# Three moves in one kernel: late sums of squares, expert weights in freed blocks, a gather ahead of scatters

## The chip, the cores and the metric

The kernel runs on one core of a Trainium2 chip. The metric is the device time of one execution in microseconds: the median over runs, here 1042.28 us before the change (three runs, 1041.61 to 1044.61).

## The reference

Three stages follow each other; the output of one is the input of the next.

```python
# 1 attention with decay: 4 batches, 8 heads, 576 positions, 64 wide
scores = q @ k.T / 8 + cum[:, None] - cum[None, :]   # cum = cumsum(log f), causal
x = softmax(scores) @ v                              # 2304 tokens of 512
# 2 SwiGLU, 1536 wide
x = (silu(x @ w_gate) * (x @ w_val)) @ w_out
# 3 one of 8 experts for each token, 1024 wide
e = argmax(x @ r_gate);  out = prob[e] * (relu(x @ w1[e]) @ w2[e])
```

All of it is float32, and the kernel splits operands into a high and a low part so that three cheaper products stand for one.

## The kernel before, in words

**Attention and SwiGLU run interleaved.** Attention is cut into 64 slots (4 batches, 4 pairs of heads, 4 slots to a pair). A slot computes scores for one item (`part1`), narrows the probabilities of the item before and sends them through a DMA transpose (`part2`, tile `pt`), and multiplies the item before that with v (`pv`, tile `px`). SwiGLU is cut into 54 units: 9 groups of 256 tokens, 6 column blocks of 256 to a group. A unit makes the gate product (`g`, 24 matmuls), the value product (`v`, 24 matmuls) and, for the unit before, the output product (`yp`, 12 matmuls). `pace` says how many slots are laid out by each unit.

**The scale of v.** Before v is narrowed to two float16 parts it is scaled by a power of two, found for a whole batch from the sum of its squares. `v_scale(b)` (line 795) loads the batch in four pieces (`vr`), squares them on ACT with a running sum (`sq`), and then calls `pow2_scale` (line 772): four matmuls `tot<-sq` on PE that add the sums over all partitions, and four small operations on DVE, through one of the three score buffers in PSUM. It is called in the 11th slot of the batch before (line 449), and `prep_v` uses the scale in the 14th.

**The gate and value weights** are kept as float16 pairs in two tiles, `wg16` and `wv16`, six blocks each. Blocks 4 and 5 also serve as landing room for raw weights while they are not yet filled.

**Routing.** After each group `fin0` copies the result `yp` to `ys` and writes it to `y_d` in DRAM. `fin1` transposes it. `fin2` finds each token's expert, its rank there, and the tables `ixf` and `ix` of token numbers by expert slot. `put_ids` scatters the numbers of tokens beyond an expert's 320 places to `id_d`, by two indirect DMAs issued from POOL; the second waits until the first has landed, since both write `id_d`. The small tiles `pos` and `tid`, which hold the scatter's addresses and values, have one buffer each that all groups share. For the last group they are copied to tiles of their own and scattered later.

**The early part of expert 0.** When group 7 of the nine (0 to 8) is routed, expert 0 surely has 128 tokens. `early_tile` (line 966) gathers them from `y_d` (tile `xg`, indirect DMA from POOL), PE transposes them into `px`, and `filler` (line 990) runs this tile through expert 0 in pieces while the last group is routed.

**Expert weights** come in eight chunks of 512 KB per expert, four for each matrix, into four landing buffers `wr`. A chunk's buffer is free again when ACT has written its high part and DVE its low part (`load_w`, lines 948 and 949). There are three homes for split matrices, used in turn: `wbuf[0]` (`whi`, `wlo`), `wbuf[1]` (`wohi`, `wolo`, the first part of the output weights' room) and `wbuf[2]`, which is allocated once SwiGLU's tiles are closed (line 1151). Expert 1's first matrix goes to `wbuf[2]`: its chunks are loaded in unit 52, and split after expert 0's tokens are transposed (line 1314). Expert 1's second matrix goes to `wbuf[0]`, where expert 0's first matrix must have been used up.

**What sets the order.** Each engine runs its own list of instructions strictly in order. The framework lays the lists out ahead of time from the program, the dependencies and its own estimate of durations, so a change in one place may move instructions of other places too. `issue_after` and `keep_in_program_order` bind a few of them.

Of the kernel before, what the change touches and what calls it, by code (L numbers as in the profile page):

```python
# [8 lines left out]
F32R = mybir.dt.float32r  # L9
F16 = mybir.dt.float16  # L10
# [17 lines left out]
def kernel(  # L28
# [108 lines left out]
    def wo_tile(fk, i, dt):  # L137
        return wo_p.tile([128, DM], dt, tag=f"wo{fk}_{i}", name="wo")

    p1 = ExitStack()  # L140
    wp = p1.enter_context(tc.tile_pool(name="wp", bufs=1, side="right"))
    wg16 = wp.tile([128, KF // 2, KD, 2, 256], F16, name="wg16")
    wv16 = wp.tile([128, KF // 2, KD, 2, 256], F16, name="wv16")
    XB = 5 * G // 128
    xr = wp.tile([128, NP, XB, 2, 128], F16, name="xr")

# [218 lines left out]
    def pv(i):  # L365
# [67 lines left out]
        for x, p in parts:  # L433
            act.activation(out=x[:, 0], in_=p, func=ACTF.Copy)
            vec.tensor_tensor(out=x[:, 1], in0=p, in1=x[:, 0], op=ALU.subtract)

    NPAIR = B * NP
    NI = 4 * NPAIR

    def slot(i):  # L440
        P = i // 4
        r = i % 4
        if i < NI:
            part1(i)
        if 0 <= i - 1 < NI:
            part2(i - 1)
        if 0 <= i - 2 < NI:
            pv(i - 2)
        if i % (4 * NP) == 10 and P // NP + 1 < B:
            v_scale(P // NP + 1)  # L450
        if P + 1 < NPAIR:
            if r == 0:
                scales(P + 1)
            if r == 1:
                prep_v(P + 1)
                if P + 2 < NPAIR:
                    load_v(P + 2)
            if r == 2:
                prep(P + 1, 0)
            if r == 3:  # L460
                prep(P + 1, 1)
                load_qk(P + 2, 1)
                load_qk(P + 3, 0)
# [17 lines left out]
    yps = {}  # L481
    hbuf = {}

    def gv(g, j, w16, name):
        ps = ps_g.tile([128, 2, G], F32, tag=name, name=name)
        x0 = g * G // 128 % XB
        for fi in range(2):
            n_ = 0
            for kk in range(KD):
                for wi, xi in ((0, 0), (0, 1), (1, 0)):  # L490
                    pe.matmul(  # L491
                        out=ps[:, fi, :],
                        lhsT=w16[:, j, kk, wi, 128 * fi:128 * fi + 128],
                        rhs=xr[:, kk, x0:x0 + 2, xi, :],
                        start=(n_ == 0),
                        stop=(n_ == 3 * KD - 1),
                    )
                    n_ += 1
        return ps
# [8 lines left out]

    def unit_g(u):
        g, j = divmod(u, KF // 2)  # L510
        gps = gv(g, j, wg16, "g")
        t = M["t"].tile([128, 2, G], F32, tag="t", name="t")
        for b, c0, c1 in spans(g):
            act.activation(  # L514
                out=t[:, :, c0:c1], in_=gps[:, :, c0:c1], func=ACTF.Tanh, scale=gscale[:, b, j:j + 1]
            )
        vec.scalar_tensor_tensor(out=t, in0=t, scalar=1.0, in1=gps, op0=ALU.add, op1=ALU.mult)  # L517
        return t

    def unit_v(u, t):  # L520
        g, j = divmod(u, KF // 2)
        vps = gv(g, j, wv16, "v")
# [7 lines left out]
        act.activation(out=hi, in_=t, func=ACTF.Copy)  # L530
# [85 lines left out]
    def fin2(g):  # L616
# [108 lines left out]
        pos = rt.tile([128, 2, 1], I32, tag="pos", name="pos")  # L725
        vec.tensor_single_scalar(out=pos, in_=pb_, scalar=float(NSLOT), op=ALU.add)
        tid = rt.tile([128, 2], I32, tag="tid", name="tid")
        vec.tensor_single_scalar(out=tid, in_=tokm[:, 2 * g:2 * g + 2], scalar=float(NT), op=ALU.add)
        if g == NG - 1:
            EP["ids"] = [EP["x0"].tile([128, 2], I32, name=x) for x in ("pos8", "tid8")]  # L730
            vec.tensor_copy(out=EP["ids"][0], in_=pos.rearrange("p i o -> p (i o)"))
            vec.tensor_copy(out=EP["ids"][1], in_=tid)
        else:
            put_ids(pos.rearrange("p i o -> p (i o)"), tid)

    def put_ids(pos, tid):
        for i in range(2):
            gp.indirect_dma_start(
                out=id_d[:, :], out_offset=bass.IndirectOffsetOnAxis(ap=pos[:, i:i + 1].bitcast(U32), axis=0),
                in_=tid[:, i:i + 1], in_offset=None, bounds_check=NSLOT - 1, oob_is_err=False,  # L740
            )
# [53 lines left out]
    def v_scale(b):  # L795
        sq = st_p.tile([128, 4], F32, tag="sq", bufs=1, name="sq")
        n = VB // 4
        for i in range(4):
            t = s_p.tile([128, 576], F32, tag="s", name="vr")[:, 0:n]
            sp.dma_start(out=t, in_=vflat[b, :, i * n:(i + 1) * n])  # L800
            act.activation(out=t, in_=t, func=ACTF.Square, accum_out=sq[:, i:i + 1])
        pow2_scale(sv[:, 0, b:b + 1], sv[:, 1, b:b + 1], [sq[:, i:i + 1] for i in range(4)])

    def unscale(b, j0, j1):
        rv = sv[:, 1, b:b + 1]
# [8 lines left out]
    raw_p = sg.enter_context(tc.tile_pool(name="raw", bufs=1, side="right"))  # L814
    c_p = sg.enter_context(tc.tile_pool(name="c", bufs=CB, side="right"))
    spare = [
        t[:, j].rearrange("p k s n -> p (k s n)").bitcast(I32) for j in (KF // 2 - 1, KF // 2 - 2) for t in (wg16, wv16)
    ]
    turnw = [0]
    free = [list(range(5))]  # L820
# [40 lines left out]
    def w_dec(j, i, h):  # L861
        f0 = 256 * j + 128 * h
        if h == 0:
            tops[j, i] = st_p.tile([128, 2], F32, tag="totw", name="totw")
        t = dec[j, i, h] = decode((w_gate, w_val)[i].rearrange("(k p) f -> p k f", p=128)[:, :, f0:f0 + 128], KD)
        act.activation(
            out=(wg16, wv16)[i][:, j, :, 0, 128 * h:128 * h + 128], in_=t, func=ACTF.Square,
            accum_out=tops[j, i][:, h:h + 1],
        )

    def w_split(j, i):
        tot = tops.pop((j, i))
        w16 = (wg16, wv16)[i]
        s1 = sw[:, 0, i, j:j + 1]
        pow2_scale(s1, sw[:, 1, i, j:j + 1], [tot[:, h:h + 1] for h in range(2)])
        for h in range(2):
            f0 = 128 * h
            src = dec.pop((j, i, h))
            hi, lo = w16[:, j, :, 0, f0:f0 + 128], w16[:, j, :, 1, f0:f0 + 128]
# [193 lines left out]
    def unit(u, between=None):  # L1073
# [5 lines left out]
        if u > 0:  # L1079
            if u - 1 < NJ:  # L1080
                upto(markw[u - 1])
            unit_o(u - 1)
            g1, j1 = divmod(u - 1, NJ)
            if g1 == NG - 1 and j1 < len(EP["w2"]):
                EP["w2"][j1]()
                if j1 == len(EP["w2"]) - 1:
                    EP["w1"] = [go() for go in load_w(1, 1, w1[1])]
            if j1 == NJ - 1:
                if g1 == 0:
                    sg.close()  # L1090
                    M.update(routing_pools())
                fin0(g1)
                if g1 == NG - 1:
                    fill.append(filler())
                late.extend([(u + 1, fin1, g1), (u + 2, fin2, g1)])
        for x in list(late):
# [10 lines left out]
    start()  # L1107
    upto(PRE0)
    scales(0)
    v_scale(0)  # L1110
    prep(0, 0)
    prep(0, 1)
    load_qk(1, 1)
# [34 lines left out]
    p1.close()  # L1148


    expert_buffers("right")
    xt_p = p2.enter_context(tc.tile_pool(name="xt", bufs=1, side="right"))
    xts.append([xt_p.tile([128, KD, CAP], F32R, name=f"x{x}1") for x in ("h", "l")])
    xg_p = p2.enter_context(tc.tile_pool(name="xg", bufs=2, side="right"))
# [126 lines left out]
    def weights(s, which):  # L1281
        src = w1 if which == 1 else w2
        return load_w(s, which, src[s]) if s < NE else load_w(s, which, src, reg["e"])
# [26 lines left out]
        return ixf[0:ROWS[t], 1, TPE * s + t:TPE * s + t + 1] if s < NE else gwo  # L1310

    xgs = {0: EP["xs"] + fetch_x(0, 1)}
    last_h, last_l = transp(xts[0], 128, xgs[0][1:], bank)
    with tc.issue_after(last_h.ins), tc.issue_after(last_l.ins):
        for f_ in EP["w1"]:
            f_()
    for s in range(NE + 1):
        nxt = s + 1 if s < NE else None
        if s == 2:
# [13 lines left out]
            xgs[nxt] = fetch_x(nxt)  # L1333
        if s == 1:
            pos_l = ix_p.tile([128, 2], I32, name="pos_l")
            tc.keep_in_program_order(vec.tensor_copy(out=pos_l, in_=EP["ids"][0]))
            put_ids(pos_l, EP["ids"][1])
        live = [go() for go in weights(nxt, 1)] if nxt is not None and s else []
        if s < NE:
            h = ht_p.tile([128, KF2, 2 * CAP], F32R, tag="h", name="h")  # L1340
# [98 lines left out]
```

## Time and profile before

| | us |
|---|---|
| median of three runs | 1042.28 |
| the profiled execution | 1036.55 |
| its span, first to last instruction | 1034.8 |
| PE busy in it | 885.4 |
| mean granted TensorE clock, share of full speed | 0.933 |

PE is the matmul engine, DVE the vector engine, ACT the scalar engine, POOL the engine that issues indirect DMAs, SP the queue that issues the others. "Granted clock" is the share of TensorE's full speed that it was allowed in a stretch; 0.5 is the lower of its two levels. A row of waits names who waited, for whom, the sum, how many times and the longest. In a timeline the bracket says how long the engine stood idle before the instruction, and what ended that.

### The profile page before, as it was taken

How to read it: one execution, taken by the hardware profiler on the slowest of the kernel's cores; microseconds unless marked ns; L12 is line 12 of the kernel's file. 1: busy time of each engine (PE TensorE's matmuls, PEld its weight loads, DVE VectorE, ACT ScalarE, POOL GpSimd, SP SyncE). 2: the span in 40 equal slices, each digit the busy share in tenths (PEclk: the TensorE clock that was granted, in tenths of full speed). 3: DMA queues.
4: the chain of work that ended last, by engine and by line, in shares of the span. 5: the costliest groups of instructions: out<-in, count | busy, mean ns of one | idle time of the engine just before them, and what ended most of it. 6: DMA issues, size and time to landing. Idle time of an engine off the chain costs nothing.

```text
span 1034.8 us, 19815 instructions
## 1 busy us (share of the span) xinstructions
PE 885.4 (86%) x7003; PEld 738.0 (71%) x7029; DVE 632.2 (61%) x1829; ACT 558.0 (54%) x1208; POOL 397.6 (38%) x473
## 2 busy tenths in 40 slices
PE   1545557989889988899899999999789899999995
PEld 0333436867667776788688878888668799899894
DVE  6999879497577575567765443234326787656440
ACT  5987988476576565556554231213225455555441
POOL 1567767364255234344444222222225643111101
PEclk9995557999999998999999999999898899999998
DMA  8897997258776768566754440203329987754430
GB/s 241 201 225 209 227 193 167 85 131 156 139 154 142 168 113 161 115 110 150 105 109 108 113 123 2 41 2 83 51 35 219 273 239 214 207 170 152 149 104 33
DMA packets 314409, 145.30 MB, mean 140 GB/s; under 512 B 279649, under 2 KB 292065, under 8 KB 314308
## 3 DMA queue, kind: packets, MB, share of 16 engines
q1 hardware_dynamic: 310016, 133.63, 55.7%
q0 software_dynamic: 4096, 10.24, 3.9%
q8 instruction: 56, 0.92, 0.4%
q14 instruction: 45, 0.37, 0.2%
q10 hardware_dynamic: 196, 0.14, 0.1%
HBM read 81.62 MB, written 10.31 MB: 89 GB/s over the span
## 4 chain that ended last, share of the span: by engine, by line
PE 42%; DMA 7%; issue 6%; ACT 3%; DVE 2%; POOL 2%; SPq 1%; POOLq 0%; DVEq 0%; ACTq 0%
PE bank L1220 9%; PE bank L1177 8%; PE yp L544 8%; PE v L491 7%; PE g L491 6%; DMA pair<-yt 1%; DMA out_dram<-o,ix 1%; POOL xg L1051 1%; PE px L381 1%; DMA qkt<-qks 1%; DMA pt<-p 1%; DMA pair<-words 1%; ACT st L321 1%; DMA wr<-in_moe_w_dram 1%; DVE st L311 1%
## 5 line engine op out<-in xcount | busy, mean ns | idle before, releaser
L491 PE MATMUL v<-xr,wv 128*128 128x256 f16 x1296 | 162.4, 281 | 0.0
L491 PE MATMUL g<-xr,wg 128*128 128x256 f16 x1296 | 161.4, 278 | 0.5 <-DMA xr<-xs 0.5
L491 PEld LDWEIGHTS <-wg 128*128 128x128 f16 x1296 | 123.6, 100 | 26.8 <-issue 9.2
L491 PEld LDWEIGHTS <-wv 128*128 128x128 f16 x1296 | 128.9, 101 | 18.9 <-issue 1.0
L346 POOL TENSOR_TENSOR p<-st,p 128x128 f16<-128x128 f32 (+3 forms) x128 | 108.7, 854 | 79.1 <-issue 52.4
L531 POOL TENSOR_TENSOR lo<-t,hi 128x512 fp32r<-128x512 f32 x54 | 71.5, 1324 | 148.6 <-ACT hi L530 123.4
L321 ACT ACTIVATE st<-st,nb,c 128x64 f32<-128x64 f32 (+4 forms) x160 | 102.6, 643 | 1.2
L381 PE MATMUL px<-vs,pt 128*128 128x64 f16 x1280 | 58.7, 203 | 41.0 <-DMA pt<-p 30.0
L343 DVE CAST p<-st 128x64 f16<-128x64 f32 (+4 forms) x160 | 71.8, 464 | 30.7 <-ACT st L321 21.9
L381 PEld LDWEIGHTS <-pt 128*128 128x128 f16 x1280 | 52.4, 106 | 52.4 <-DMA pt<-p 35.1
L514 ACT ACTIVATE t<-g,gscale 128x512 f32<-128x512 f32 (+3 forms) x72 | 39.3, 571 | 75.5 <-PE g L491 75.5
L256 PE MATMUL ps<-qkt 128*128 128x64 f16 (+2 forms) x192 | 56.7, 311 | 25.9 <-DMA qkt<-qks 11.3
L357 POOL TENSOR_TENSOR p<-st,p 128x64 f16<-128x64 f32 (+1 forms) x128 | 54.2, 425 | 61.5 <-DVE p L343 30.6
L1220 PE MATMUL bank<-whi,h 128*128 128x512 f32 x200 | 66.9, 400 | 4.8 <-ACT h L1182 4.8
L983 POOL DMA_INDIRECT out_dram<-o,ix x24 | 26.6, 1110 | 113.8 <-ACT o L1222 71.2
L311 DVE CUSTOM_DVE_ANT_0 st<-ps,zero 128x64 f32<-128x64 f32 (+3 forms) x160 | 55.6, 376 | 24.2 <-PE ps L264 21.0
L517 DVE SCALAR_TENSOR_TENSOR t<-t,g 128x512 f32<-128x512 f32 x54 | 36.9, 684 | 54.3 <-ACT t L514 54.2
L530 ACT ACTIVATE hi<-t 128x512 fp32r<-128x512 f32 x54 | 33.8, 625 | 60.8 <-DVE t L524 60.8
L949 DVE TENSOR_TENSOR wlo<-wr,whi 128x1024 fp32r<-128x1024 f32 x48 | 57.7, 1245 | 14.1 <-ACT whi L948 12.3
L257 PE MATMUL ps<-qkt 128*128 128x64 f16 (+2 forms) x192 | 59.9, 315 | 0.0
L544 PE MATMUL yp<-wohi,hi 128*128 128x512 f32 x144 | 59.7, 414 | 0.0
L1177 PE MATMUL bank<-xh,whi 128*128 128x320 f32 (+1 forms) x192 | 58.9, 309 | 0.5 <-ACT xh L93 0.5
(300 smaller groups left out, 2274.2 us busy)
## 6 DMA issues: line engine op xcount, KB each, us to landing
wr<-in_moe_w_dram SPq DMA_DIRECT2D x72, 512.0 KB
vr<-in_v_dram SPq DMA_DIRECT2D x16, 288.0 KB
qk_in<-in_q_dram SPq DMA_DIRECT2D x32, 128.0 KB
qk_in<-in_k_dram SPq DMA_DIRECT2D x32, 128.0 KB
v_in<-in_v_dram SPq DMA_DIRECT2D x32, 128.0 KB
y_d<-ys SPq DMA_DIRECT2D x6, 512.0 KB
wg<-in_moe_w_gate_dram SPq DMA_DIRECT2D x5, 512.0 KB
raw<-in_moe_w_val_dram SPq DMA_DIRECT2D x5, 512.0 KB
```

The source lines that it names most:

```text
L257: pe.matmul(out=ps[:, o:o + n], lhsT=lq, rhs=qkt[:, 2, k0:k1], start=False, stop=False, skip_group_check=True)
L311: vec.tensor_tensor_reduce(out=sts[m][:, k0 - 64:k1 - 64], in0=ps[:, o:o + n], in1=zero.to_broadcast([128, n]), scale=1.0, scalar=init, op ...
L321: act.activation(out=sts[m], in_=sts[m], func=ACTF.Exp, scale=c[:, 0:1], bias=nb[:, m:m + 1], accum_out=sm[:, m, hh:hh + 1],)
L343: vec.tensor_copy(out=flat[:, o + 64:o + 64 + n], in_=src)
L346: gp.tensor_tensor(out=flat[:, o1:o1 + n - 64], in0=src[:, 64:n], in1=flat[:, o + 128:o + 64 + n], op=ALU.subtract)
L381: pe.matmul(out=px[:, 128 * m + 64 * hh:128 * m + 64 * hh + 64], lhsT=pm[:, o + ph * last + c, :], rhs=vs[:, hh, c, vh, :], start=(c == 0 ...
L491: pe.matmul(out=ps[:, fi, :], lhsT=w16[:, j, kk, wi, 128 * fi:128 * fi + 128], rhs=xr[:, kk, x0:x0 + 2, xi, :], start=(n_ == 0), stop=(n_ ...
L531: last["lo"] = gp.tensor_tensor(out=lo, in0=t, in1=hi.bitcast(F32), op=ALU.subtract)
L544: pe.matmul(out=yps[g][i], lhsT=hx[:, fi, 128 * i:128 * i + 128], rhs=wo[fk][wx], start=(j == 0 and n_ == 0), stop=(j == KF // 2 - 1 and n ...
L949: (eng or vec).tensor_tensor(out=l_, in0=t, in1=h_.bitcast(F32), op=ALU.subtract)
L1177: pe.matmul(out=p, lhsT=w[wi][:, kk, 128 * fk:128 * fk + 128], rhs=x[xi][:, kk, c0:CAP], start=(n_ == 0), stop=(n_ == 3 * KD - 1),)
L1220: pe.matmul(out=p[0:m, :], lhsT=hx, rhs=wx, start=(n_ == 0), stop=(n_ == len(prods) - 1))
```

## The change

`v_scale` now loads and squares as before and returns a function that does the rest. For batch 1 it is called at once; for batches 2 and 3 it is called two slots later. The first four blocks of the gate and value weights get a pool of their own; when the last unit is done, expert 1's first matrix takes their place and is split there, behind the last `hi`, and the loads of its second matrix follow at once. Group 7's scatter addresses are held in tiles of their own, and its two scatters are issued behind the last `lo`.

```diff
+    JA = 4
+    wpa = ctx.enter_context(tc.tile_pool(name="wpa", bufs=1, side="right"))
+    w16a = [wpa.tile([128, JA, KD, 2, 256], F16, tag=x, name=x) for x in ("wga", "wva")]
+
+    def w16_of(i, j):
+        return w16a[i][:, j] if j < JA else w16b[i][:, j - JA]
+
     p1 = ExitStack()
     wp = p1.enter_context(tc.tile_pool(name="wp", bufs=1, side="right"))
-    wg16 = wp.tile([128, KF // 2, KD, 2, 256], F16, name="wg16")
-    wv16 = wp.tile([128, KF // 2, KD, 2, 256], F16, name="wv16")
+    w16b = [wp.tile([128, KF // 2 - JA, KD, 2, 256], F16, name=x) for x in ("wgb", "wvb")]
...
         if i % (4 * NP) == 10 and P // NP + 1 < B:
-            v_scale(P // NP + 1)
+            vsum.append(v_scale(P // NP + 1))
+            if P < NP:
+                vsum.pop()()
+        if i % (4 * NP) == 12 and vsum:
+            vsum.pop()()
...
-        if g == NG - 1:
-            EP["ids"] = [EP["x0"].tile([128, 2], I32, name=x) for x in ("pos8", "tid8")]
-            vec.tensor_copy(out=EP["ids"][0], in_=pos.rearrange("p i o -> p (i o)"))
-            vec.tensor_copy(out=EP["ids"][1], in_=tid)
+        if held:
+            EP["ids", g] = (pos, tid)
         else:
-            put_ids(pos.rearrange("p i o -> p (i o)"), tid)
+            put_ids(pos, tid)
...
-        pow2_scale(sv[:, 0, b:b + 1], sv[:, 1, b:b + 1], [sq[:, i:i + 1] for i in range(4)])
+        return lambda: pow2_scale(sv[:, 0, b:b + 1], sv[:, 1, b:b + 1], [sq[:, i:i + 1] for i in range(4)])
...
                     EP["w1"] = [go() for go in load_w(1, 1, w1[1])]
+            elif g1 == NG - 1 and j1 == NJ - 1:
+                wbuf.append([wpa.tile([128, 4096], F32R, tag=x, name=x) for x in ("wga", "wva")])
+                with tc.issue_after(last["hi"].ins):
+                    for f_ in EP["w1"]:
+                        f_()
+                EP["w12"] = [go() for go in load_w(1, 2, w2[1])]
...
                 fin0(g1)
                 if g1 == NG - 1:
+                    with tc.issue_after(last["lo"].ins):
+                        put_ids(*EP["ids", NG - 2])
                     fill.append(filler())
...
-    expert_buffers("right")
...
-    last_h, last_l = transp(xts[0], 128, xgs[0][1:], bank)
-    with tc.issue_after(last_h.ins), tc.issue_after(last_l.ins):
-        for f_ in EP["w1"]:
-            f_()
+    transp(xts[0], 128, xgs[0][1:], bank)
...
-        live = [go() for go in weights(nxt, 2)] if nxt is not None else []
+        if s == 0:
+            live = EP["w12"]
+        else:
+            live = [go() for go in weights(nxt, 2)] if nxt is not None else []
```

On PE, in the slots where batch 2's scale is made, the kernel before has the four `tot<-sq` apart from each other; the third stands among the rank counts (`rk`, five small matmuls of the routing), ahead of the last of these and of the next scores (`ps<-qkt`).

```order
L776 MATMUL tot<-sq,onesf 128x1
L653 LDWEIGHTS ones
L653 MATMUL rk<-oh,ones 128x8
L256 LDWEIGHTS qkt
L256 MATMUL ps<-qkt 128x448
```

In the changed kernel the four stand in one piece, two slots further on, behind the last products of probabilities and v (`px`) of an item and ahead of the next pair's scale (`tot<-am`) and of a unit's value product.

```order
L387 LDWEIGHTS pt
L387 MATMUL px<-vs,pt 128x64
L791 MATMUL tot<-sq,onesf 128x1 x4
L791 MATMUL tot<-am,onesf 128x2
L503 LDWEIGHTS wvb
L503 MATMUL v<-xr,wvb 128x256
```

Batch 3's four move in the same way: two stood around the start of a gate product and two among the `px` products just ahead of a value product; now they stand in one piece behind a whole item's 25 `px` products. The squares themselves (`vr` on ACT) are not asked later, only what uses their sums; for batch 3 three of them now stand in one piece, ahead of the next pair's squares and of a unit's tanh (`t<-g`), where before two stood a little earlier and two right ahead of that tanh.

On POOL, at the end of SwiGLU, the kernel before has group 7's two scatters (`id_d`), one `lo` and then the early gather (`xg` by `ix_9793`).

```order
L738 DMA id_d<-tid,pos 16384x1 x2
L531 TENSOR_TENSOR lo<-t,hi 128x512
L1051 DMA xg<-y_d,ix_9793 128x512
L1237 IOTA thr 1x128
L1242 IOTA ii 1x128
```

In the changed kernel the early gather comes first, and the scatters follow the last `lo`, ahead of the gathers of the expert stage (`xg` by `ix`).

```order
L543 TENSOR_TENSOR lo<-t,hi 128x512 x4
L1066 DMA xg<-y_d,ix_9792 128x512
L1259 IOTA thr 1x128
L1264 IOTA ii 1x128
L543 TENSOR_TENSOR lo<-t,hi 128x512
L753 DMA id_d<-tid_9788,pos_9787 16384x1 x2
L1066 DMA xg<-y_d,ix 128x512
```

Both scatters have moved past the early gather and the last `lo`.

On ACT, behind the last unit's `hi`, the kernel before copies the last group's result (`ys`) and goes on with its transposes; the four splits of expert 1's first matrix come much later, behind `xh`.

```order
L514 ACTIVATE t<-g,gscale 128x512
L93 ACTIVATE xh_8999<-px 128x4x128
L530 ACTIVATE hi<-t 128x512
L574 ACTIVATE ys<-yp 128x512
L612 ACTIVATE yt<-ps 128x512
```

In the changed kernel these splits (`wga`) stand between `hi` and `ys`; on DVE three of the four low parts stand ahead of its half of `ys`, and one behind it.

```order
L526 ACTIVATE t<-g,gscale 128x512
L93 ACTIVATE xh_9004<-px 128x4x128
L542 ACTIVATE hi<-t 128x512
L963 ACTIVATE wga<-wr 128x1024 x4
L586 ACTIVATE ys<-yp 128x512
L624 ACTIVATE yt<-ps 128x512
```

The four splits have moved ahead of `ys`. On SP the write of `y_d` for the last group now has three loads of expert 1's second matrix ahead of it and one behind it; before, all four were issued later, at the start of the expert stage.

## Rows read from the trace of the kernel before

**Rows 1.** The page: span and the busy time of the engines.

```profile
span 1034.8 us, 19815 instructions
...
PE 885.4 (86%) x7003; PEld 738.0 (71%) x7029; DVE 632.2 (61%) x1829; ACT 558.0 (54%) x1208; POOL 397.6 (38%) x473
```

**Rows 2.** The waits of PE, 250 to 728 us: total, times, longest.

```profile
PE tot L776 <- ACT vr L801: 7.7, 3, 3.9
PE px L381 <- DMA pt<-p: 7.7, 8, 1.8
```

**Rows 3.** Busy time by stretch, engine by engine; then granted clock, DMA share, GB/s.

```profile
276.00:284.00 8.00, 7.95 (x87) 6.61 (x89) 5.62 (x30) 3.18 (x7) 1.14 (x1) 0.83 0.50 34
...
391.00:396.00 5.00, 1.11 (x10) 1.11 (x11) 0.00 (x0) 1.94 (x5) 1.09 (x1) 0.87 1.09 212
396.00:402.00 6.00, 6.00 (x30) 4.47 (x31) 4.03 (x13) 4.22 (x12) 1.17 (x2) 0.54 1.03 171
...
747.20:753.30 6.10, 6.09 (x20) 4.87 (x21) 1.44 (x2) 1.23 (x2) 1.80 (x3) 0.51 0.21 73
753.30:773.00 19.70, 19.31 (x105) 14.84 (x103) 6.62 (x41) 4.61 (x9) 2.90 (x4) 1.00 0.21 32
...
784.00:808.00 24.00, 24.00 (x161) 21.78 (x161) 16.61 (x33) 11.91 (x18) 12.76 (x13) 1.00 0.98 222
...
813.20:818.00 4.80, 4.80 (x12) 3.83 (x13) 4.16 (x11) 1.57 (x3) 4.21 (x4) 0.50 1.05 188
```

**Rows 4.** The chain that ended last, 380 to 412 us: start, us, what.

```profile
389.24 4.74 DMA vr<-in_v_dram
...
396.33 5.12 PE v L491 x24
401.45 2.85 PE yp L544 x12
404.30 2.63 PE g L491 x24
```

**Rows 5.** The waits of PE, 728 to 830 us.

```profile
PE px L1062 <- DMA xg<-y_d,ix: 6.7, 1, 6.7
PE bank L1220 <- ACT h L1182: 4.8, 1, 4.8
PE bank L1062 <- DMA xg<-y_d,ix: 4.1, 1, 4.1
```

**Rows 6.** Timeline of POOL, 728 to 743 us: start, us, what, [idle before].

```profile
730.71 1.05 POOL L738 DMA_INDIRECT id_d<-tid,pos  x1 [3.16 <-DVE eq L680]
739.94 0.97 POOL L738 DMA_INDIRECT id_d<-tid,pos  x1 [8.18 <-DMA id_d<-tid,pos]
...
742.37 1.06 POOL L1051 DMA_INDIRECT xg<-y_d,ix  x1 [0.16 <-issue]
```

**Rows 7.** Timeline of DVE, 728 to 745 us.

```profile
734.62 0.15 DVE L969 CAST ix<-ixf 128x1 int32<-128x1 f32 x1
...
744.03 0.17 DVE L728 TENSOR_SCALAR tid<-tokm 128x2 int32<-128x2 f32 x1 [9.20 <-DMA id_d<-tid,pos]
```

**Rows 8.** Timeline of ACT, 770 to 790 us.

```profile
778.86 3.89 ACT L948 ACTIVATE whi<-wr 128x1024 fp32r<-128x1024 f32 x4
```

**Rows 9.** Timeline of SP, 750 to 790 us.

```profile
781.20 3.77 SPq L939 DMA_DIRECT2D wr<-in_moe_w_dram  x4
```

**Rows 10.** The chain that ended last, 725 to 830 us.

```profile
757.70 2.83 DMA y_d<-ys
...
769.18 0.98 POOL xg L1051
...
790.15 8.14 DMA pair<-words
...
804.31 6.66 DMA wr<-in_moe_w_dram
...
813.18 4.63 PE bank L1220 x10
```

More of the change, by code (lines that the diff above doesn't have):

```diff
@@ L435, in pv @@
             vec.tensor_tensor(out=x[:, 1], in0=p, in1=x[:, 0], op=ALU.subtract)
+    vsum = []
     NPAIR = B * NP
@@ L482, with gv @@
     hbuf = {}
-    def gv(g, j, w16, name):
+    def gv(g, j, i, name):
+        w16 = w16_of(i, j)
         ps = ps_g.tile([128, 2, G], F32, tag=name, name=name)
@@ L492, in gv @@
                         out=ps[:, fi, :],
-                        lhsT=w16[:, j, kk, wi, 128 * fi:128 * fi + 128],
+                        lhsT=w16[:, kk, wi, 128 * fi:128 * fi + 128],
                         rhs=xr[:, kk, x0:x0 + 2, xi, :],
@@ L510, in unit_g @@
         g, j = divmod(u, KF // 2)
-        gps = gv(g, j, wg16, "g")
+        gps = gv(g, j, 0, "g")
         t = M["t"].tile([128, 2, G], F32, tag="t", name="t")
@@ L521, in unit_v @@
         g, j = divmod(u, KF // 2)
-        vps = gv(g, j, wv16, "v")
+        vps = gv(g, j, 1, "v")
         for b, c0, c1 in spans(g):
@@ L529, in unit_v @@
         lo = M["h"].tile([128, 2, G], F32R, tag="lo", name="lo")
-        act.activation(out=hi, in_=t, func=ACTF.Copy)
+        last["hi"] = act.activation(out=hi, in_=t, func=ACTF.Copy)
         last["lo"] = gp.tensor_tensor(out=lo, in0=t, in1=hi.bitcast(F32), op=ALU.subtract)
@@ L724, in fin2 @@
         vec.tensor_tensor(out=pb_, in0=pb_, in1=ov_, op=ALU.mult)
-        pos = rt.tile([128, 2, 1], I32, tag="pos", name="pos")
-        vec.tensor_single_scalar(out=pos, in_=pb_, scalar=float(NSLOT), op=ALU.add)
-        tid = rt.tile([128, 2], I32, tag="tid", name="tid")
+        held = g >= NG - 2
+        pos, tid = [
+            EP["x0"].tile([128, 2], I32, name=f"{x}{g}") if held else rt.tile([128, 2], I32, tag=x, name=x)
+            for x in ("pos", "tid")
+        ]
+        vec.tensor_single_scalar(
+            out=pos.rearrange("p (i o) -> p i o", o=1), in_=pb_, scalar=float(NSLOT), op=ALU.add
+        )
         vec.tensor_single_scalar(out=tid, in_=tokm[:, 2 * g:2 * g + 2], scalar=float(NT), op=ALU.add)
-        if g == NG - 1:
-            EP["ids"] = [EP["x0"].tile([128, 2], I32, name=x) for x in ("pos8", "tid8")]
-            vec.tensor_copy(out=EP["ids"][0], in_=pos.rearrange("p i o -> p (i o)"))
-            vec.tensor_copy(out=EP["ids"][1], in_=tid)
+        if held:
+            EP["ids", g] = (pos, tid)
         else:
-            put_ids(pos.rearrange("p i o -> p (i o)"), tid)
+            put_ids(pos, tid)
     def put_ids(pos, tid):
@@ L816 @@
     spare = [
-        t[:, j].rearrange("p k s n -> p (k s n)").bitcast(I32) for j in (KF // 2 - 1, KF // 2 - 2) for t in (wg16, wv16)
+        w16_of(i, j).rearrange("p k s n -> p (k s n)").bitcast(I32) for j in (KF // 2 - 1, KF // 2 - 2) for i in range(2)
     ]
@@ L866, in w_dec @@
         act.activation(
-            out=(wg16, wv16)[i][:, j, :, 0, 128 * h:128 * h + 128], in_=t, func=ACTF.Square,
+            out=w16_of(i, j)[:, :, 0, 128 * h:128 * h + 128], in_=t, func=ACTF.Square,
             accum_out=tops[j, i][:, h:h + 1],
@@ L872, in w_split @@
         tot = tops.pop((j, i))
-        w16 = (wg16, wv16)[i]
+        w16 = w16_of(i, j)
         s1 = sw[:, 0, i, j:j + 1]
@@ L878, in w_split @@
             src = dec.pop((j, i, h))
-            hi, lo = w16[:, j, :, 0, f0:f0 + 128], w16[:, j, :, 1, f0:f0 + 128]
+            hi, lo = w16[:, :, 0, f0:f0 + 128], w16[:, :, 1, f0:f0 + 128]
             act.activation(out=hi, in_=src, func=ACTF.Copy, scale=s1)
@@ L1109 @@
     scales(0)
-    v_scale(0)
+    v_scale(0)()
     prep(0, 0)
@@ L1335 @@
             pos_l = ix_p.tile([128, 2], I32, name="pos_l")
-            tc.keep_in_program_order(vec.tensor_copy(out=pos_l, in_=EP["ids"][0]))
-            put_ids(pos_l, EP["ids"][1])
+            tc.keep_in_program_order(vec.tensor_copy(out=pos_l, in_=EP["ids", NG - 1][0]))
+            put_ids(pos_l, EP["ids", NG - 1][1])
         live = [go() for go in weights(nxt, 1)] if nxt is not None and s else []
```

## The prediction

> **What bounds the kernel now.** I read the page first, then the waits of PE in two halves of the span, then the busy time of the stretches around the longest waits, then the chain through them, and last the timelines of the engines that PE waits for. PE is busy for 885.4 of 1034.8 us, DVE as the next engine for 632.2 [rows 1], so time comes off this kernel where PE stands still or runs slowly, and nowhere else. The reader is to see three things in the rows.
>
> First, PE's long waits that touch the change are few: 7.7 us for the squares of v (three waits, the longest 3.9) [rows 2], 6.7 for the early gather, 4.8 for ACT's `h` in expert 1, 4.1 for the expert stage's first gathers [rows 5]. Second, a long wait is paid twice. In the stretch behind the 3.9 the granted clock is 0.54, behind the 6.7 it is 0.51, behind the 4.8 it is 0.50, all at about the lower of the two levels; behind the squares of batch 2 it is 0.83 over 8 us [rows 3]. So the price of a wait is its length plus the stretch behind it times the share of speed that was missing. Third, between 753 and 773 the DMA engines are 0.21 busy, between 784 and 808 they are 0.98 busy [rows 3].
>
> **Term A, the sums two slots later.** The work is the same: sixteen matmuls and a few operations on tiny operands, now in two places instead of spread. What goes is PE standing behind squares that stand behind loads. In batch 3 PE stops at about 391, the loads land at 389.24 + 4.74 = 394.0 [rows 4], and PE goes on at half speed. The price there is 3.9 + 6.0 x (1 - 0.54) = 6.7. Batch 2 has the other two waits, 7.7 - 3.9 = 3.8, and 8.0 x (1 - 0.83) = 1.4 of slow clock, 5.2 together. The upper end of A is 11.9.
>
> The lower end is 0, and a little below if the new order hurts (last rival). What is late next in batch 3: ACT still stands before the same loads until 394.0, since the squares were not moved. PE has behind its old wait a value product and an output product. At full speed these take 2.63 (a gate product has as many matmuls) + 2.85 = 5.5 [rows 4], which covers 391.0 to 396.5. Then comes a gate product that needs the tanh of the one before, and ACT now has the next pair's two squares ahead of that tanh. I take 2 us for that, so 4.7 are left in batch 3, and 9.9 in all. Of this I count 7: up to the end of attention PE also waits eight times for transposed probabilities, 7.7 us in all [rows 2], and that chain through ACT, POOL and DMA has no shorter work than before.
>
> **Term C, the gather ahead of the scatters.** On POOL the second scatter waits 8.18 us for the first, and the early gather starts at 742.37, although its index was ready at 734.8 [rows 6, 7]. In the change only one `lo` stands before it. I allow 1 us for that: start at about 735.8, 6.6 earlier, so that the tile lands when PE, which stopped at 747.2 - 6.7 = 740.5, comes to it. A second wait must go with it, and does: DVE stood 9.20 us before `tid`, the one buffer that the scatters still read, with the last unit's work queued behind it [rows 7]. Groups 7 and 8 now have tiles of their own. The gain is at most 6.7 + 6.1 x (1 - 0.51) = 9.7 [rows 3, 5]. Against it stand the four splits put ahead of `ys`: ACT needs 3.89 for such four [rows 8] from the last `hi` on, while PE needs 2.85 for the last output product, so `ys` is about 1.0 late. With 0.2 for the last `lo` I take C = 8.5. Its lower end is 5 (third rival).
>
> The scatters cost nothing where they are now. The first is issued behind the last `lo`, at about 745.5 (the result's write at 757.7 [rows 10] less 8.5, less the output product's 2.85 and some 1 us for `lo`), the second 8.2 and one issue later, over by 756. The expert stage's gathers start at 769.18 [rows 10] less 8.5 = 760.7. If the cover of 5 us were gone, every microsecond would count. The 4.1 of waiting for these gathers stays, as routing, gather and PE all move together.
>
> **Term B, expert 1's matrix in the freed blocks.** Four splits leave the start of the expert stage for the end of SwiGLU (counted in C). With them four loads of 512 KB, issued from 781.20 on [rows 9], go to about 746. At 222 GB/s they are 2.1 MB / 222 = 9.4 us of transfers, taken from a stretch that is 0.98 busy into one with a share of 0.21 [rows 3]. The 4.8 us wait for `h` ends a chain of two transfers, the words of expert 2's tokens (8.14) and the last chunk of its first matrix (6.66) [rows 10], both in the full stretch. The upper end is the wait and its slow clock, 4.8 + 4.8 x (1 - 0.50) = 7.2 [rows 3, 5]. The lower end is 0: expert 2's loads still wait for landing buffers, which are freed by the splits of expert 1's second matrix, which wait for expert 0's first products, in both kernels. If the two transfers lose a third of their 14.8 us, that is 4.9, and the wait is gone with its slow clock; expert 2's low parts on DVE are late next, for which I take 2 back. B = 5.
>
> The weights in four tiles instead of two cost nothing, as no instruction is added. Two copies of ids on DVE go (0.17 for an operation of that size [rows 7]), off the path.
>
> **The sum.** A 7 + C 8.5 + B 5 = 20.5. The profiled execution took 1036.55 us, 1.75 of it around its span; it would take 1016. The median of the runs is 5.73 above it, and I take the difference from the median: 1042.28 - 20.5 = 1021.8, so 1022. All upper ends give 28.8 and 1013.5; all lower ends give 5 and 1037.
>
> **The rivals.**
>
> *Attention takes A back.* PE's waits for the squares would only turn into waits for transposed probabilities and for the tanh, as ACT is held by the same loads. For it speaks that ACT's loads are not earlier; against it, that DVE did nothing at all from 391 to 396 [rows 3], so all engines gain there. Then 13.5 are left: 1029. Chance 0.20.
>
> *The last group's result stands in line.* SP issues the write of `y_d` behind three loads. Alone it takes 2.83 [rows 10]. Three loads of 0.52 MB at 222 GB/s take 7.1; issued at 757.7 - 8.5 = 749.2 the write lands at 759.1, 1.6 before the gathers at 760.7. At the 171 GB/s of another full stretch [rows 3] and with the fourth load's bytes among them, four times 3.1, it lands at 764.4. Then C loses 3.7, and the time is 1026. Chance 0.12, since DMA is idle there otherwise. The Trainium skill says, on the page "DMA: Bandwidth & Descriptors" under "Queues, rings and completion order", that each DMA engine consumes a queue's descriptors in ring order; by that rule the write's bytes do come behind the loads' bytes. No row of before has such a write behind loads.
>
> *Everything shows.* All three terms reach their upper ends: 1014. For it speaks that most waits fall in stretches where other engines stand too. Chance 0.10.
>
> *The new order costs more than the change gives.* From batch 2's sums to the end of attention the lists of all engines are laid out anew, the transposes on SP among them. If probabilities reach PE late, each new wait like that of batch 3 costs 6.7. A is then 0, 13.5 are left, and from three such waits on (20.1) the kernel is slower, 1049 with three. It decides between two and three. Against it: none of the eight waits of this kind is longer than 1.8 now [rows 2]. Chance 0.08.
>
> **How the numbers follow.** The forecast has 0.50 and by itself spans 1018 to 1026. With 'everything shows' below, the line before `y_d` beside it and most of the case without A above, 1013 to 1034 holds a little over 0.8. About 0.3% or 3.1 us is what a measurement of this kernel can tell from no change. The first four cases are faster by more, 0.92 together, of which I take 0.03 off for mixtures of their poor ends: faster 0.89, same 0.04, slower 0.07.
>
> **What would show it.** For C: the early gather's bracket on POOL no longer names a scatter, PE's wait before `px` is under 1 us and the clock behind it near full. For A: no wait of PE for `vr` behind 255 us, and fewer microseconds from there to the end of attention by about 7. For B: `wr` loads between 745 and 760, PE's wait before the second product of expert 1 under 2 us. The prediction is wrong if PE's waits in attention grow as those for `vr` go, if `ys` is written less than 6 us earlier, or if the wait for the expert stage's first gathers grows from 4.1.

## The result, and the profile after

The changed kernel takes 1029.3 us (median of four runs, 1028.4 to 1030.1), beside 1041.9 for the kernel before (four runs). The ratio is 0.988, with a 95% interval of 0.986 to 0.991: 12.6 us less. The forecast was 1022, with a range of 1013 to 1034.

The page of the changed kernel, its span and the busy time of the engines, answers to [rows 1]:

```profile
span 1028.3 us, 19837 instructions
...
PE 886.9 (86%) x7029; PEld 734.8 (71%) x7029; DVE 623.6 (61%) x1827; ACT 558.2 (54%) x1208; POOL 397.3 (39%) x473
```

PE works as long as before; only its idle time can have changed. This profiled execution took 1030.1 us and that of before 1036.55, which is 5.4 below the median of before. So the two traces differ by only 6.5 us, and the sizes below are taken from several executions.

The waits of PE from 250 to 728 us (total, times, longest), for [rows 2]:

```profile
PE px L387 <- DMA pt<-p: 20.6, 13, 6.5
PE ps L641 <- ACT lgp L638: 3.3, 1, 3.3
PE yp L556 <- POOL lo L543: 2.3, 2, 1.7
PE tot L791 <- ACT jk L195: 0.9, 2, 0.5
```

The waits for `vr` are gone, all three. In their place PE waits 20.6 us for transposed probabilities instead of 7.7, and two of these waits are long, 6.5 and 5.0 us. In the chain that ended last (start, us, what) they stand behind two long landings of `pt`, the time from SP's issue until the data is there:

```profile
272.34 10.42 DMA pt<-p
...
358.12 11.61 DMA pt<-p
```

At the end of SwiGLU the order is the one that was forecast. The timeline of POOL, for [rows 6]:

```profile
737.23 1.08 POOL L1066 DMA_INDIRECT xg<-y_d,ix  x1 [0.15 <-issue]
...
746.63 1.82 POOL L753 DMA_INDIRECT id_d<-tid,pos  x1 [0.16 <-issue]
754.16 0.98 POOL L753 DMA_INDIRECT id_d<-tid,pos  x1 [5.71 <-DMA id_d<-tid,pos]
761.15 0.98 POOL L1066 DMA_INDIRECT xg<-y_d,ix  x1 [6.01 <-DVE cnt L718]
```

The early gather waits for no scatter, the two scatters behind it are issued before the expert stage's gathers, and these start 8.0 us earlier than in [rows 10]. The waits of PE from 728 to 830 us, for [rows 5], no longer have the early gather in them, and the one for `h` has fallen from 4.8 to 0.8:

```profile
PE bank L1077 <- DMA xg<-y_d,ix: 4.9, 1, 4.9
PE bank L1242 <- ACT h L1204: 0.8, 1, 0.8
...
```

The chain there still has the same two transfers, at 6.51 and 8.41 us where [rows 10] has 6.66 and 8.14:

```profile
793.22 6.51 DMA wr<-in_moe_w_dram
...
803.06 8.41 DMA pair<-words
```

### The profile page after: what moved, and what is told of

It reads as the page before. It is cut to its first block, busy times and chain, and to the rows that moved or that the text cites. A ratio compares the mean times of both kernels' runs of the same rounds, so it can differ in the third digit from the quotient of the medians.

```text
span 1028.3 us, 19837 instructions
## 1 busy us (share of the span) xinstructions
PE 886.9 (86%) x7029; PEld 734.8 (71%) x7029; DVE 623.6 (61%) x1827; ACT 558.2 (54%) x1208; POOL 397.3 (39%) x473
## 4 chain that ended last, share of the span: by engine, by line
PE 40%; DMA 19%; issue 11%; DVE 8%; ACT 5%; SPq 3%; POOL 3%; POOLq 0%; DVEq 0%; ACTq 0%
PE yp L556 10%; PE v L503 9%; PE g L503 9%; DMA pt<-p 5%; DMA out_dram<-o,ix 5%; PE bank L1199 3%; DMA qkt<-qks 2%; PE bank L1242 2%; PE px L387 2%; DMA pair<-words 2%; DMA xg<-y_d,ix 1%; ACT st L327 1%; DVE st L317 1%; DVE p L349 1%; SPq L366 1%
## 5 line engine op out<-in xcount | busy, mean ns | idle before, releaser
L503 PE MATMUL g<-xr,wga 128*128 128x256 f16 x864 | 105.4, 276 | 0.6 <-DVE sw L801 0.6
L503 PE MATMUL v<-xr,wva 128*128 128x256 f16 x864 | 105.6, 275 | 0.0
L503 PEld LDWEIGHTS <-wga 128*128 128x128 f16 x864 | 82.4, 99 | 18.5 <-issue 7.4
L503 PEld LDWEIGHTS <-wva 128*128 128x128 f16 x864 | 84.2, 100 | 10.3 <-issue 0.3
L262 PE MATMUL ps<-qkt 128*128 128x64 f16 (+2 forms) x192 | 56.3, 311 | 20.1 <-DMA qkt<-qks 9.8
L265 PE MATMUL ps<-cum,nc 128*128 128x64 bf16 (+2 forms) x192 | 58.9, 314 | 0.0
L556 PE MATMUL yp<-wohi,lo 128*128 128x512 f32 x144 | 57.0, 397 | 0.7 <-POOL lo L543 0.7
L1206 DVE SCALAR_TENSOR_TENSOR h<-bank,h 128x64 fp32r<-128x64 f32 (+2 forms) x128 | 33.3, 304 | 39.9 <-ACT h L1204 39.9
```

The lines of the kernel that those rows point to most:

```text
L262: pe.matmul(out=ps[:, o:o + n], lhsT=lq, rhs=qkt[:, 1, k0:k1], start=True, stop=False, skip_group_check=True)
L265: pe.matmul(out=ps[:, o:o + n], lhsT=pk, rhs=cum3[:, k0 - 64:k1 - 64], start=False, stop=(k1 <= d0), skip_group_check=True,)
L503: pe.matmul(out=ps[:, fi, :], lhsT=w16[:, kk, wi, 128 * fi:128 * fi + 128], rhs=xr[:, kk, x0:x0 + 2, xi, :], start=(n_ == 0), stop=(n_ == ...
L556: pe.matmul(out=yps[g][i], lhsT=hx[:, fi, 128 * i:128 * i + 128], rhs=wo[fk][wx], start=(j == 0 and n_ == 0), stop=(j == KF // 2 - 1 and n ...
```

## The experiments

Chips differ: the kernel before has a median of 1033.4 us beside the first four runs, 1033.8 beside the next four, 1032.7 and 1028.7 beside the last two pairs. So each run is told as a ratio to before on its own chip, with its 95% interval, and in microseconds of that before.

### The three parts alone

The first part alone on the kernel before:

```diff
-            v_scale(P // NP + 1)
+            vsum.append(v_scale(P // NP + 1))
+            if P < NP:
+                vsum.pop()()
+        if i % (4 * NP) == 12 and vsum:
+            vsum.pop()()
...
```

> The kernel before with the first part of the change alone: the sums of squares of batches 2 and 3 two slots later. Come-back theory (the saved waits return as waits of PE for transposed probabilities, because the transposes of q and k now go out earlier and share the DMA engines with those of the probabilities): within 3 us of before, 1039 to 1044 us; PE's waits for pt between 250 and 728 us sum to 15 us or more, against 7.7, with at least one over 4 us near 283; none for vr. Rival (the new waits in the profile were an accident of one execution, and the part is worth what was predicted): 7 us less, 1035, and waits for pt under 10 us.

Measured: 0.998 (0.9955 to 1.0012), -1.6 us. Waits for `pt` 17.0 us, the longest 6.1, none for `vr`. The saved waits come back as the come-back theory says, though not by the mechanism that it names (see the transpose of q and k below), and the rival's 7 us lies outside the interval.

The third part alone:

```diff
+        held = g >= NG - 2
...
                 if g1 == NG - 1:
+                    with tc.issue_after(last["lo"].ins):
+                        put_ids(*EP["ids", NG - 2])
```

> The kernel before with the third part alone: groups 7 and 8 keep their positions and ids in tiles of their own, and group 7's scatters go behind the last low part, so the early gather comes before them. The theory that this part is worth what was predicted: 8.5 us and about 1.0 more, since the four splits that delay ys belong to the second part: 1032.5, between 1031 and 1035. Rival (the gather's gain is partly the second part's, or is given back at the start of the expert stage): 1036 or more.

Measured: 0.992 (0.989 to 0.995), -8.3 us. The first theory's 9.5 lies within the interval of 5.5 to 11, and the rival's 6 or less just reaches into it; the stretches decide. The busy time of the stretch from the `ys` of group 7 to that of group 8 (start and end, length, busy us of PE, PEld, DVE, ACT, POOL with their instructions, granted clock, DMA share, GB/s), kernel before:

```profile
701.00:756.00 55.00, 48.30 (x340) 40.03 (x340) 19.61 (x60) 13.71 (x21) 12.90 (x13) 0.91 0.32 63
```

the third part alone:

```profile
698.20:743.60 45.40, 45.40 (x341) 38.11 (x340) 19.31 (x58) 13.82 (x22) 11.98 (x12) 1.00 0.34 76
```

and the changed kernel:

```profile
702.40:748.70 46.30, 46.30 (x344) 38.84 (x343) 22.15 (x61) 17.41 (x25) 12.76 (x12) 1.00 0.36 75
```

The stretch takes 55.0 us before: PE idles for 6.7 of them and is busy longer, at a granted clock of 0.91. It takes 45.4 with the third part alone, without any idle time and at full clock, and 46.3 where the four splits of the second part stand ahead of `ys`. In the traces it is 53.5 to 55.0 without the third part, 45.4 with it alone and 46.3 or 46.4 with both.

The second part alone:

```diff
-    expert_buffers("right")
...
+                with tc.issue_after(last["hi"].ins):
+                    for f_ in EP["w1"]:
+                        f_()
+                EP["w12"] = [go() for go in load_w(1, 2, w2[1])]
```

> The kernel before with the second part alone: expert 1's first matrix split into the freed gate weight blocks, its second matrix loaded early. Theory: about 3 us less at the second product of expert 1, of which later waits for h and lower clock take 2 or more back, and the four splits ahead of ys cost 1: within 3 us of before, 1039 to 1044. Rival (the second part carries the whole rest of the gain, as the first gives nothing): 5 us less or more, 1037 or below.

Measured: 0.9986 (0.996 to 1.001), -1.4 us, not told apart from nothing; the rival's 5 or more lies outside the interval. Where the forecast 5 went is seen by stretches of the expert stage, cut at equal distances from its first gather. The second and third stretch of the run with the first part alone, which has the old weights:

```profile
789.70:809.70 20.00, 16.60 (x88) 14.78 (x87) 15.52 (x26) 11.84 (x15) 14.95 (x10) 0.91 1.03 265
809.70:839.70 30.00, 30.00 (x172) 27.51 (x171) 22.21 (x46) 15.82 (x22) 15.37 (x16) 1.00 0.89 254
```

and of this run:

```profile
796.10:816.10 20.00, 20.00 (x119) 18.41 (x118) 14.48 (x29) 11.34 (x15) 15.78 (x11) 1.00 1.02 286
816.10:846.10 30.00, 26.88 (x138) 23.25 (x137) 22.94 (x44) 15.12 (x20) 12.73 (x14) 0.94 0.86 240
```

PE's 3.4 us of idle time and the clock of 0.91 leave the second stretch and come back as 3.1 us and 0.94 in the third. There it waits for `h` of the next expert, 1.6 for ACT's half and 1.5 for DVE's. The wait has moved on by one expert. The three parts alone add up to 11.3 us, near the 12.6 of the whole.

### Which batch, and the whole again

```diff
-            if P < NP:
+            if P < 2 * NP:
```

> The changed kernel, but with batch 2's sums asked at once, as before; only batch 3's are two slots later. Come-back theory: the wait of 6.5 us near 283 goes and batch 2's waits for vr (3.8 us in all) return, so the expert stage is reached some 3 to 5 us earlier: 1024 to 1027. Rival (the long wait near 283 is not due to the moved sums): slower than the changed kernel by about 4, 1033.

Measured: 0.9905 (0.987 to 0.994), -10 us. Both long waits for `pt` are gone, the one near 370 too, although batch 3's sums are still late; two waits for `vr` are back (4.0 us), and the waits for `pt` sum to 6.4, the longest 1.9. The time can't be told apart from the changed kernel's (next), so neither a gain nor the rival's loss is shown; the long waits do hang on the moved sums of batch 2.

> The changed kernel once more, beside the same runs of before as the next three. Come-back theory: about 12 us less than before, as in its first runs; again a wait of PE of 5 us or more for pt near 283 us, and 15 us or more for pt between 250 and 728 us. Rival (those waits were an accident of one execution): under 10 us for pt, and no wait over 3.

Measured: 0.988 (0.985 to 0.992), -12 us, the first result again on another chip. Waits for `pt` 19.2 us, the longest, 6.2, between 262 and 292 us: no accident.

The changed kernel without its first part (`v_scale` as before):

> The changed kernel without its first part: all sums of squares asked at once. Come-back theory: the part is worth 0 to 3 us, so this is at most 3 us slower than the changed kernel; three waits for vr return (6 to 8 us) and the waits for pt fall to 8. Rival (the part is worth the 7 us predicted): 7 us slower than the changed kernel.

Measured: 0.992 (0.989 to 0.995), by the medians 2.5 us over the run above it. Waits for `vr` 7.2 us, for `pt` 7.6. So the first part is worth about 2 us by both ways of isolating it (1.6 and 2.5), and the uncertainty reaches from nothing to about 5.

### Two tries that didn't gain

The four splits behind `ys`, the loads behind the write of `y_d`:

```diff
-                with tc.issue_after(last["hi"].ins):
+                    with tc.issue_after(last["ys"].ins):
```

> The changed kernel, but the four splits of expert 1's first matrix stand behind the last group's ys instead of ahead of it, and the loads of the second matrix behind the write of y_d. If the splits cost what was predicted there, ys comes 1.0 us sooner behind the last output product, PE's wait for the expert stage's first gathers falls from 4.9 to about 3.9, and the time is 1 us less, near what five rounds can tell. Rival (these splits are needed sooner than ys, or the loads lose by being later): same time or 1 us more, with longer waits for h in the expert stage.

Measured: 0.991 (0.988 to 0.994), no gain. `ys` does come 1.0 us sooner (45.3 us for the stretch), but PE waits 5.9 instead of 4.9 to 5.4 for the first gathers and longer for DVE's `h`. The forecast cost of the splits is there, and it isn't worth moving.

The transpose of q and k held back, to find what makes `pt` land late:

```diff
+        if (P, hh) == (7, 1):
+            held_t.append(go)
...
+        if i == 28:
+            with tc.issue_after(ptx["pt"].ins):
+                held_t.pop()()
```

> The changed kernel, but the transpose of q and k of one head pair (the second half of pair 7, which goes out at about 276 us behind two transposes of probabilities) is issued behind the next item's two transposes. Collision theory (the probabilities land late because that transpose shares the DMA engines with them): the wait near 283 falls from 6.5 us to under 2.5, and the time is 3 to 7 us under the changed kernel's. Rival 1 (the two loads of v ahead of them, or the probabilities' transposes themselves, are what takes long): the wait stays over 5, no gain. Rival 2 (the collision only moves on to the next scores): the wait goes, PE waits as long for qkt, no gain.

Measured: 0.989 (0.986 to 0.992), the changed kernel's time. The collision theory fell: the wait stays, as its first rival has it. What that rival names, the loads of v or the transposes themselves, is tested below. SP's timeline in this run (start, us that the issue took, what):

```profile
269.80 0.38 SPq L583 DMA_DIRECT2D g_d<-gw  x1
270.27 2.72 SPq L372 DMA_TRANSPOSE pt<-p  x2
...
285.23 1.59 SPq L239 DMA_TRANSPOSE qkt<-qks  x1
```

and its chain of waits:

```profile
270.27 10.74 DMA pt<-p
```

The transpose of q and k is out of the way until 285, and `pt` still takes 10.74 us (PE's longest wait for it is 6.9). Another row stands out: directly ahead of the slow transposes SP issues `g_d`, a group's gate values, 1 KB in pieces of four bytes. In the kernel before, SP's list has it the other way round:

```profile
269.65 1.02 SPq L800 DMA_DIRECT2D vr<-in_v_dram  x2
270.79 3.36 SPq L360 DMA_TRANSPOSE pt<-p  x2
274.24 0.53 SPq L562 DMA_DIRECT2D g_d<-gw  x1
...
280.83 3.52 SPq L231 DMA_TRANSPOSE qkt<-qks  x1
```

In the changed kernel the write has gone ahead, here and (behind it `pt` with 11.61 us) at 357.48:

```profile
270.74 1.02 SPq L815 DMA_DIRECT2D vr<-in_v_dram  x2
271.86 0.38 SPq L574 DMA_DIRECT2D g_d<-gw  x1
272.34 2.78 SPq L366 DMA_TRANSPOSE pt<-p  x2
...
357.48 0.54 SPq L574 DMA_DIRECT2D g_d<-gw  x1
358.12 1.30 SPq L366 DMA_TRANSPOSE pt<-p  x1
```

The median landing of a `pt`, over those that the trace times, is 3.2 us there. The run with the held transpose has one more such pair: PE waits 7.9 us there for a transpose of q and k that SP issued 2.4 us behind another `g_d`.

### The small write

Nothing of the write's place in the code had changed; the planner that lays out the lists put it two places earlier. With batch 2's sums at their old place SP issues it behind the two transposes again (they at 269.19, it at 272.95 us, in the run with only batch 3's sums late), so the moved sums are what pulled it ahead. That PE's list closed up behind them and routing came out sooner is how I read it.

The kernel before has such pairs too, with a transpose of q and k behind the write. Its SP and PE's weight loads (start, us, what, idle before):

```profile
360.98 0.43 SPq L562 DMA_DIRECT2D g_d<-gw  x1
362.23 4.03 SPq L231 DMA_TRANSPOSE qkt<-qks  x1
...
370.27 0.10 PEld L256 LDWEIGHTS <-qkt 128*128 128x128 f16 x1 [0.42 <-DMA qkt<-qks]
```

That transpose lands 8.0 us behind its issue, but the weight loads waited only 0.42 us for it. So the slow landing is not new; the change put transposes behind the write that PE was waiting for.

The next run keeps the gate values of groups 0 to 6 in a tile of their own and writes them behind attention:

```diff
-        rows_out(g_d, g, gw)
+        gq.append(g)
+        while g >= 6 and gq:
+            with tc.issue_after(ptx["pt"].ins):
+                rows_out(g_d, gq[0], gws[:, gq.pop(0)])
```

> The changed kernel, but the routed tokens' gate values (g_d, 1 KB of four-byte values per group) are kept in a tile of their own and written to DRAM behind attention's last transpose, not in each group. The rest of SP's list is the same. Small-write theory (the two long landings, 10.4 and 11.6 us, are those of the transposes of probabilities that SP issues right behind g_d; in the kernel before they stand ahead of it): PE's longest wait for pt falls from 6.5 us to under 3, their sum from 19 to 20 us to under 11, and the time is 7 to 11 us under the changed kernel's on the same chip: 1011 to 1015 where that has 1022. Rival (the transposes are slow by themselves or through the loads of v ahead of them, and the long waits are only what stood behind the old ones): the waits stay, same time within 2 us.

Its waits of PE from 250 to 728 us, the first two:

```profile
PE px L390 <- DMA pt<-p: 12.3, 16, 2.4
PE yp L559 <- ACT hi L545: 12.1, 1, 12.1
```

The mechanism holds: no wait for `pt` is longer than 2.4 us, 12.3 in all. The loads of v still stand ahead of the transposes near 270, so they are not what takes long. The time doesn't follow: 0.999 (0.996 to 1.002), with a new wait of 12.1 us. Eight writes now stand in a row at 570 to 585, and what SP issues among and behind them lands late, by the chain:

```profile
572.94 14.76 DMA wr<-in_moe_w_dram
587.76 6.95 DMA xr<-xs
```

ACT stands 17.5 us before the splits of these loads, with a unit's `hi` queued behind. I take it for the same effect on other transfers; the changed kernel with the writes spread (below) has no writes there, and no longer has the wait.

> The changed kernel, but ACT's queue issues the write of the gate values (g_d), at the same place in the program. If what holds the transposes is that they stand behind the write in SP's queue, the long waits for pt go as with the late write: under 11 us in all, 7 to 11 us less time. If it is the write itself on the DMA engines, whoever issues it, the waits stay at 6 us and the time at the changed kernel's. ACT's own issues may cost up to 0.5 us each where PE waits for ACT.

The edit is `q=act` for `sp` in the write's four calls. Measured: 0.9935 (0.991 to 0.996), no better than the changed kernel, and the long wait stays:

```profile
PE px L387 <- DMA pt<-p: 21.0, 12, 8.7
```

So it isn't the place in SP's queue: behind a write by ACT's queue at 267.7 SP's transposes are held too, and now take 11.79 us to issue:

```profile
269.29 11.79 SPq L366 DMA_TRANSPOSE pt<-p  x2
```

The Trainium skill says on its page "DMA: Bandwidth & Descriptors", section "Issuing engines are not separate DMA queues", that DMAs of different issuing engines end on the same sixteen DMA engines and interleave there. This run agrees, with the 11.79 us above.

Last, the late writes spread over two places with nothing behind them, in the changed kernel and in the kernel before:

```diff
+        for x in [gq.pop(0) for _ in range({5: 3, 6: 4, 7: 1, 8: 1}.get(g, 0))]:
+            with tc.issue_after(ptx["pair"].ins):
+                rows_out(g_d, x, gws[:, x])
```

> The changed kernel with the gate values of groups 0 to 6 written behind attention again, now not all behind its last transpose, where eight writes in a row held expert 0's loads, but three groups' behind the transposes of group 5's result and four behind group 6's, where SP has nothing else for some 40 us. Small-write theory: PE's waits for pt stay as in the first try (12 us, longest under 3), its wait of 12 us for hi near 590 goes, and group 4's ys keeps its 7 us: 6 to 9 us under the changed kernel, 0.980 to 0.983 of before. Rival (the gain up to group 4 was one execution's luck, or comes back elsewhere): 0.988 as for the changed kernel.

> The kernel before with the same late writes of the gate values and nothing else. If the writes cost time only where the change put them ahead of transposes of probabilities, this is within 2 us of before, and with the writes out of the way the change is worth 18 to 21 us. Rival (they cost before as well, where transposes of q and k stood behind them): 3 to 6 us less than before, and the change is worth about what it was, 12 to 15.

Measured: the changed kernel with late writes 0.986 (0.982 to 0.990), -14.3 us, the best ratio of all; the kernel before with them 1.001 (0.999 to 1.004). The waits are as expected:

```profile
PE px L390 <- DMA pt<-p: 10.2, 10, 2.5
```

The 12.1 us wait is gone. But the gain over the changed kernel's 0.988 is about 2 us, not 6 to 9, and the intervals overlap. The kernel before stays within 2 us, as the first theory has it; between the two kernels with late writes lie 15 us, at the upper end of the rival's 12 to 15 and under the expected 18 to 21. So the write is shown as the cause of the two long waits, and a gain in time from moving it is not shown.

## Why the prediction was right, and where not

| | forecast | measured alone | by the traces |
|---|---|---|---|
| A, sums later | 7 | 1.6 (-1.2 to 4.7) | idle -1.7 |
| C, gather first | 8.5 | 8.3 (5.5 to 11) | 55.0 to 46.3 with the splits |
| B, freed blocks | 5 | 1.4 (-1.2 to 4.0) | idle 3.4 there, 3.1 one expert later |
| sum | 20.5 | 11.3 | |

The time lay in the range, and at the number of the rival "Attention takes A back" (1029), to which I gave 0.20. Only C carried it there: two of the three terms failed, and C alone would give 1033.6, just inside the range. That the time met the rival's 1029 is luck, since that rival had A at nothing and B at its full 5.

**C was right in mechanism and size.** Its upper end of 9.7 is the 9.6 us of the third part alone. The 1.0 that I took off for the splits ahead of `ys` is the 0.9 between 45.4 and 46.3. The wait and the slow clock behind it went together, as [rows 3] had let one expect.

**A failed at the step "Of this I count 7".** The waits for `vr` went as worked out, and the waits for `pt` grew: what I had named as the sign of being wrong. I had kept a margin of 3 for that chain because it "has no shorter work than before". It got longer, by a neighbour that I had not looked at: SP's list, where the write of the gate values went ahead of the transposes (10.42 and 11.61 us to land). From group 0's `ys` to group 4's, PE idles 27.4, 23.9, 26.6 and 28.1 us in four executions of the old order of sums, 25.0, 23.9, 25.1 and 25.1 in four of the new one, 24.1 in the old one with the writes late, and 19.8 and 20.4 in the new one with the writes late. With the write where it was, the part removes 1.7 us of idle time on average, which is less than the four executions of one order differ by. With the writes late in both orders it removes about 4 (24.1 less 20.1), nearer to the 7.7 less 2 of the forecast, but the 24.1 is a single execution and also lies among those of the old order.

The rival's own reason, ACT held by the same loads, is not what the runs show.

**A's second failed step is the slow clock**, 4.2 us of its upper end of 11.9. I took the clock behind each wait from one execution as if it belonged to the wait. Here is that stretch of attention for the kernel before:

```profile
235.40:541.50 306.10, 278.67 (x2710) 226.69 (x2723) 198.53 (x716) 183.17 (x472) 128.28 (x184) 0.96 0.69 135
```

and for the changed kernel without its first part, which has the same order of sums:

```profile
235.50:535.60 300.10, 272.00 (x2710) 222.37 (x2723) 197.20 (x716) 183.22 (x472) 128.81 (x184) 0.99 0.71 138
```

PE idles about as long in both (27.4 and 28.1), with a granted clock of 0.96 and 0.99: 6 us between two executions of one order, perhaps of two chips, none of it in idle time. What a few short waits cost in clock over such a stretch can't be read from a single trace. With the new order and late writes it is

```profile
234.80:529.80 295.00, 275.20 (x2728) 222.29 (x2725) 196.47 (x716) 183.45 (x473) 129.99 (x184) 0.98 0.74 140
```

**B failed at the step "if the two transfers lose a third of their 14.8 us".** They take 14.9 now. The wait for `h` did go, and in the run of B alone its length came back at the next expert (3.4 and 3.1 us), where I had taken 2 back for what is "late next". How I read it: ACT and DVE have as much to split as before, so one chunk earlier is one chunk earlier for one expert only.

**The rival of `y_d` behind three loads** came in part. The write behind the loads did get slower, 8.5 us to land instead of 2.83, by the changed kernel's list of DMAs (KB each, median us to landing over those that the trace times):

```profile
y_d<-ys SPq DMA_DIRECT2D x6, 512.0 KB, 8.5
```

Issued at 750.50, it landed some 2 us before the gathers, as in the rival's milder case (759.1), and the gathers' start shows no cost: they start 12.4 us behind the last `ys`, beside 13.1 before. Their wait grew from 4.1 to 4.9, one of my signs of being wrong, yet it is only 0.8, and I put it down to `ys` being later against PE's work: it is 3.8 with the third part alone.

**What stays open.** What the late writes are worth in time: they take about 5 us of idle time from the changed kernel's attention in two traces, and the 2 us of time are uncertain by some 5. And what in the DMA engines holds the transposes: the runs vary the write's place and queue, not the size of its pieces.

## What to carry to other kernels

When a change lets one engine's list close up, read the list of the DMA queue too, for what else has come earlier: a 1 KB write that nobody waits for brought two waits of 6.5 and 5.0 us here, where 7.7 us of waits for the squares had gone. A wait for a chain that repeats (here one expert after the other) may only move on by one turn if the chain itself gets no shorter. And a clock loss read from one trace belongs to a wait only where it goes and comes with the wait in several.

## What the runs showed of the hardware

A DMA transpose of probabilities issued 0.5 to 0.7 us behind a write of 256 four-byte values to DRAM landed after 10.4, 11.6 and 10.7 us instead of a median of 3.2, and with ACT issuing the write two of them took 11.79 us to issue. Meanwhile the DMA engines move next to nothing; busy time in the changed kernel, behind the write at 271.86 us:

```profile
276.00:278.00 2.00, 0.27 (x3) 0.00 (x0) 0.82 (x6) 1.97 (x6) 0.33 (x1) 1.00 1.97 46
278.00:280.00 2.00, 0.00 (x0) 0.00 (x0) 1.78 (x4) 1.70 (x5) 1.06 (x2) 0.92 1.26 15
```

The DMA share is over 1 at 46 and 15 GB/s, and PE stands still. In the kernel before, behind the write at 360.98 us, it is much the same for the DMA engines, while PE has work:

```profile
363.00:365.00 2.00, 2.00 (x28) 1.84 (x26) 2.00 (x9) 1.97 (x6) 1.00 (x1) 1.00 1.75 60
```

A plain load of weights among eight such writes took 14.8 us.
